# The 32x32 inverses of a delta-rule attention stage on VectorE: one triangular solve of 32 rows, or two of 16 rows and products for the corner

## The chip, the cores and the metric

The kernel runs on one core of a Trainium2 chip. The metric is the time of one execution on the device in microseconds. The core's engines work side by side, each through its own list of instructions in a fixed order: TensorE (matrix products, PE in the profile), VectorE (DVE), ScalarE (ACT), GpSimd (POOL) and SyncE (SP, which here only issues transfers). An instruction that needs another engine's result waits on a semaphore, and everything behind it in its engine's list waits with it.

## What is computed

Three layers in a row, all float32: attention by the delta rule, then two layers of feed-forward networks. Only the first is touched by the change.

```
for t in range(S):                      # S = 768, batch 4, heads 8, head size 48
    y[t]  = q[t] @ state
    v_old = state.T @ k_n[t]            # k_n = k / (|k| + 1e-6)
    state = state + beta[t] * outer(k_n[t], v[t] - v_old)
x = moe(x)                              # 3072 tokens, 8 experts, top 2, 384 -> 1024 -> 384
return (h * clip(h + 3, 0, 6) / 6) @ w_out   # h = x @ w_in, 384 -> 2048 -> 384
```

## The kernel before

The 768 steps of the delta rule are not taken one by one. They are cut into chunks of 64, and a tile `n` holds one chunk of two batches (128 partitions) and all 8 heads; there are 24 tiles. Within a chunk the steps depend on one another through the Gram matrix of the keys, K K^T, below its diagonal. They are resolved at once by the inverse of a unit lower triangular matrix of 64x64 per head. Its two diagonal blocks of 32x32 are inverted on VectorE; the corner is made on TensorE from them (`merge1`, `merge2`).

`gram` multiplies the keys on TensorE into a PSUM tile `gm` (two buffers). ScalarE then reads it: a copy of the corner into `goff`, and a copy, masked to one half, into `gd` (L222, L223). VectorE adds the other half to `gd` (L224; called a Gram sum below) and thereby frees the buffer of `gm` for the Gram after the next. Eight Gram sums (four tiles) fill one `gd`.

`inverse_ops(g)` builds the list of VectorE's work for four tiles, 128 matrices of 32x32: `gd` is transposed into `A` so that each partition holds one whole 32x32 matrix along its free dimension (`A[t, i]`, row t, column i); the norms are made from the diagonal; `A` is scaled (L292); `T` becomes the inverse times the factors in 31 steps. Step jj multiplies column jj of A below the diagonal with row jj of T (L296, `tmp`), and subtracts the product from T below (L304). The subtraction is cut into pieces, so that the next step's row is ready first. Then `T` is transposed into `Xc` and `Yc` (L321, L322). There are six inverses, g = 0 to 5; they are called the first to the sixth below.

For a tile, `merge1` (L347) multiplies `goff` with `Xc`, `merge2` (L368) multiplies with `Yc`, and VectorE assembles the result into `x` (L370, called x below). One PSUM tile `mg` serves both, so the next tile's `merge1` waits for the x before it. `solve` (L399) uses x; `ks` and `update` carry the state from a tile to the tile after next, with ScalarE's copies between them; `output` (L422) makes y. `v_norm` (L377) multiplies v with the norms on GpSimd, two instructions per tile. Tiles two at a time pass through this while the Gram of tiles eight further on is made.

The order is written by hand, apart from VectorE's inverses. These stand in a list with planned costs in us; `run(t)` is called after each piece of TensorE's work with that piece's planned time, times 0.95, and takes from the list what this credit pays for. The tail with the transposes comes when the rest is done. `weave` lays the router's small instructions (`rt_...`) between the inverse's. So a planned cost sets only where in VectorE's list an instruction stands. `late` and `flush` put a Gram sum or an x right behind the piece that made it.

Of the kernel before, what the change touches and what calls it, by code (L numbers as in the profile page):

```python
# [7 lines left out]
F32 = mybir.dt.float32  # L8
# [4 lines left out]
ALU = mybir.AluOpType  # L13
AX = mybir.AxisListType
# [77 lines left out]
def emit_attention(ctx, tc, q, k, v, beta, const, rt, moe):  # L92
    nc = tc.nc
    early = ExitStack()
    pr = early.enter_context(tc.tile_pool(name="at_r", bufs=1, side="right"))
    pk = ctx.enter_context(tc.tile_pool(name="at_k", bufs=1))
    wk = ctx.enter_context(tc.tile_pool(name="at_w", bufs=2))
# [45 lines left out]
    goff, gd, inv, rows, vt, x64, beta_t = {}, {}, {}, {}, {}, {}, {}  # L143
# [59 lines left out]
    def gram(n, hh, what="both"):  # L203
        g, j = divmod(n, 4)
        lo, hi = dict(both=(0, 128), g=(64, 128), m=(0, 64))[what]
        if (j, hh) == (0, 0) and lo < hi and hi == 128:
            gd[g] = pr.tile([128, 32, 32], F32, tag="gd", name="gd", bufs=1)
        if hh == 0 and hi == 128:
            goff[n] = wk.tile([128, NH, 32], F32, tag="goff", name="goff", bufs=11)
        gm = ps2.tile([128, 4, 128], F32, tag="gm", name="gm")  # L210
        for h in range(4):
            for b in range(2):
                m = mq[b][n % NM][st[b], 4 * hh + h]
                nc.tensor.matmul(gm[tok[b], h, lo:hi], lhsT=m[:, 1, :], rhs=m[:, lo // 64:hi // 64, :],  # L214
                                 start=True, stop=True)
        hs = slice(4 * hh, 4 * hh + 4)
        if lo == 0:
            for b in range(2):
                nc.scalar.copy(out=mq[b][n % NM][tok[b], hs, 0, :], in_=gm[tok[b], :, 0:64])
        if hi == 128:  # L220
            d = gd[g][:, 8 * j + 4 * hh:8 * j + 4 * hh + 4, :]
            nc.scalar.mul(out=d, in_=gm[:, :, 64:96], mul=m0)  # L222
            nc.scalar.copy(out=goff[n][:, hs, :], in_=gm[:, :, 64:96])  # L223
            late.append(lambda: nc.vector.scalar_tensor_tensor(  # L224
                out=d, in0=gm[:, :, 96:128], scalar=m1, in1=d, op0=ALU.mult, op1=ALU.add))
        if lo == 0 and hh:
            if n < 6:
                masks.append(n)
            else:
                mask(n)  # L230
# [3 lines left out]
    def mask(n):  # L234
        for b in range(2):
            m = mq[b][n % NM][tok[b], :, 0, :]
            nc.gpsimd.affine_select(out=m, in_=m, pattern=[[0, NH], [1, CH]], compare_op=ALU.is_gt,
                                    fill=0.0, base=0, channel_multiplier=-1)

    def inverse_ops(g):  # L240
        ops = []
        A = pr.tile([128, 32, 32], F32, tag="A", name="A", bufs=1)
        T = pr.tile([128, 32, 32], F32, tag="T", name="T", bufs=1)
        tmp = [pr.tile([128, 256], F32, tag=f"tmp{i}", name="tmp", bufs=1) for i in range(2)]
        sm = wk.tile([128, 8, 32], F32, tag="sm", name="sm", bufs=2)
        rw = wk.tile([128, 32], F32, tag="rows", name="rows", bufs=2)
        rows[g] = rw
        Af, Tf = A.rearrange("p t i -> p (t i)"), T.rearrange("p t i -> p (t i)")
        n2, s, r, nn, gg = [sm[:, i, :] for i in range(5)]

        y, u = sm[:, 5, :], sm[:, 6, :]
        V = nc.vector

        def head():
            nc.gpsimd.memset(T, 0.0)
            V.transpose(out=A, in_=gd[g].rearrange("p j t -> p t j"))
            V.tensor_copy(out=n2, in_=Af[:, 0:1024:33])
            if g == 0:
                nc.scalar.sqrt(s, n2)

        if g == 0:
            norm = [
                lambda: V.tensor_scalar(out=nn, in0=s, scalar1=1e-30, scalar2=None, op0=ALU.add),
                lambda: V.reciprocal(out=r, in_=nn),
                lambda: V.tensor_tensor(out=r, in0=n2, in1=r, op=ALU.mult),
                lambda: V.tensor_tensor(out=s, in0=s, in1=r, op=ALU.add),
                lambda: V.tensor_scalar(out=nn, in0=s, scalar1=0.5, scalar2=1e-6, op0=ALU.mult, op1=ALU.add),
            ]
        else:
            norm = [  # L270
                lambda: V.tensor_scalar(out=u.bitcast(I32), in0=n2.bitcast(I32), scalar1=1, scalar2=None,
                                        op0=ALU.logical_shift_right),
                lambda: V.tensor_scalar(out=y.bitcast(I32), in0=u.bitcast(I32), scalar1=-1.0,
                                        scalar2=float(0x5F3759DF), op0=ALU.mult, op1=ALU.add),
            ] + [
                lambda: V.scalar_tensor_tensor(out=u, in0=y, scalar=-0.5, in1=n2, op0=ALU.mult, op1=ALU.mult),
                lambda: V.tensor_tensor(out=u, in0=u, in1=y, op=ALU.mult),
                lambda: V.scalar_tensor_tensor(out=y, in0=u, scalar=1.5, in1=y, op0=ALU.add, op1=ALU.mult),
            ] * 3 + [
                lambda: V.tensor_tensor(out=s, in0=n2, in1=y, op=ALU.mult),  # L280
                lambda: V.tensor_scalar(out=nn, in0=s, scalar1=1e-6, scalar2=None, op0=ALU.add),
            ]
        norm += [
            lambda: V.tensor_tensor(out=r, in0=nn, in1=nn, op=ALU.mult),
            lambda: V.reciprocal(out=r, in_=r),
            lambda: V.transpose(out=rw, in_=nn),
            lambda: V.tensor_tensor(out=gg, in0=beta_t[g], in1=r, op=ALU.mult),
            lambda: V.tensor_copy(out=Tf[:, 0:1024:33], in_=gg),
        ]

        def scale():
            V.tensor_tensor(out=A, in0=A, in1=gg.unsqueeze(2).to_broadcast([128, 32, 32]), op=ALU.mult)  # L292

        def product(jj):
            m, w = 31 - jj, jj + 1
            nc.vector.tensor_tensor(  # L296
                out=tmp[jj % 2][:, 0:m * w].rearrange("p (t k) -> p t k", k=w),
                in0=A[:, jj + 1:32, jj:jj + 1].to_broadcast([128, m, w]),
                in1=T[:, jj:jj + 1, 0:w].to_broadcast([128, m, w]), op=ALU.mult)

        def subtract(jj, lo, hi):
            if lo < hi:
                w = jj + 1
                nc.vector.tensor_tensor(  # L304
                    out=T[:, lo:hi, 0:w], in0=T[:, lo:hi, 0:w],
                    in1=tmp[jj % 2][:, (lo - w) * w:(hi - w) * w].rearrange("p (t k) -> p t k", k=w), op=ALU.subtract)

        def step(jj):
            product(jj)
            if jj:  # L310
                subtract(jj - 1, (jj + 33) // 2, 32)
            subtract(jj, jj + 1, jj + 2)
            subtract(jj, jj + 2, (jj + 34) // 2)

        def tail():
            if g == NG - 1:
                second()
            X = wk.tile([128, 32, 32], F32, tag="Xc", name="Xc", bufs=1)
            Y = wk.tile([128, 32, 32], F32, tag="Yc", name="Yc", bufs=1)
            inv[g] = (X, Y)  # L320
            nc.vector.transpose(out=X.rearrange("p j t -> p t j"), in_=T)  # L321
            nc.vector.transpose(out=Y.rearrange("p j k -> p k j"), in_=T.rearrange("p t k -> p k t"))  # L322

        ops.append((1.6, head))
        ops.extend((0.23, fn) for fn in norm)
        ops.append((1.1, scale))
        for jj in range(31):
            ops.append((0.25 + 0.0021 * (31 - jj) * (jj + 1), lambda jj=jj: step(jj)))
        ops.append((None, tail))
        return ops  # L330

# [3 lines left out]
    def second():  # L335
        other = ps2.tile([128, NH, 32], F32, tag="gm", name="mg2")
        nc.vector.memset(other, 0.0)
        mgs.update({NT - 3: other, NT - 1: other})
# [187 lines left out]
    for i in range(8):  # L526
        if TA > 1:
            flush()
        if i + TA < 8:
            trans(*divmod(i + TA, 2))  # L530
        flush()
        gram(*divmod(i, 2), "g")
        warm(P1[i])
# [4 lines left out]
    for m in range(4):  # L538
        load_v(m)
        if m < 2:  # L540
            load_k(m)
    pend += inverse_ops(0)
    run(4.0)
    rt.setup(wk, ps2)
    for n in range(4):
        for hh in range(2):
            gram(n, hh, "m")
            warm(P2)
            run(PQ)
    trans(4, 0)  # L550
    for i in range(8, 16):
        n, hh = divmod(i, 2)
# [29 lines left out]
    for n in range(0, NT - 4, 2):  # L582
        a = n + LA
# [84 lines left out]
    n = NT - 4  # L668
# [956 lines left out]
```

## Time and profile before

| | |
|---|---|
| median of 3 runs | 1234.47 us (1234.45 to 1235.84) |
| span of the profiled execution | 1245.6 us |
| TensorE, busy | 1163.7 us (93%) |
| VectorE, busy | 711.4 us (57%) |
| ScalarE, busy | 548.2 us (44%) |
| GpSimd, busy | 311.6 us (25%) |

The profile is of one execution by itself. No other time than its span is recorded for it; the span is 11.1 us longer than the median of the runs. The attention stage takes about the first 345 us; the six inverses begin (transpose of gd into A) at 20.61, 59.15, 108.63, 160.71, 211.95 and 266.61 us, and the last one's transposes end at 313.8 us. A time such as 101.47 is the start of an instruction, in us from the start of the span. The rows below say in brackets how long the engine sat idle before an instruction, and what ended it.

### The profile page before, as it was taken

Reading aid. Unit: us, or ns where it says so; the run is one execution under the profiler, and the core shown is the slowest. Engines: PE = TensorE matmul, PEld = TensorE weight load, DVE = VectorE, ACT = ScalarE, POOL = GpSimd, SP = SyncE. Lnnn points to the kernel's source line nnn. Section 1 sums busy time; section 2 is a strip of 40 time slices with the busy share of each in tenths; the row PEclk is TensorE's granted clock in tenths of the full one; section 3 lists DMA queues with packets and bytes.
Section 4 is the critical chain, followed back from the end, with each engine's and each line's share of the span. In section 5 each row is a group of like instructions: output and inputs, shape, how many; then the busy total and the mean of one; then the engine's idle time right before and its main releaser. Section 6 shows DMA issues by size and latency. Waiting matters only on the chain. (4 is left out here: it accounts for less than half of the span.)

```text
span 1245.6 us, 26717 instructions
## 1 busy us (share of the span) xinstructions
PE 1163.7 (93%) x10743; PEld 1051.9 (84%) x10760; DVE 711.4 (57%) x1923; ACT 548.2 (44%) x1133; POOL 311.6 (25%) x399
## 2 busy tenths in 40 slices
PE   7798888787878999999999999989999999999998
PEld 4476767665757999999999999978989898998988
DVE  7988789879363777675757453436242433425150
ACT  5776777763453433232324233337242433434150
POOL 7242244555244513232231313015000000000000
PEclk9998899988889999999999999999999999999999
DMA  4634334322325545444534321262202010110000
GB/s 85 103 79 92 66 73 92 73 40 42 91 77 190 159 161 173 164 144 155 188 136 160 116 90 56 67 200 78 70 7 64 13 60 17 45 33 2 24 1 26
DMA packets 146530, 109.47 MB, mean 88 GB/s; under 512 B 110104, under 2 KB 131941, under 8 KB 145638
## 3 DMA queue, kind: packets, MB, share of 16 engines
q1 hardware_dynamic: 137446, 86.39, 25.1%
q0 software_dynamic: 8448, 19.70, 4.9%
q8 instruction: 85, 1.39, 0.5%
q10 hardware_dynamic: 512, 1.67, 0.4%
q14 instruction: 39, 0.32, 0.1%
HBM read 82.43 MB, written 26.08 MB: 87 GB/s over the span
## 5 line engine op out<-in xcount | busy, mean ns | idle before, releaser
L1197 PE MATMUL yp<-w2h,ht 128*128 128x384 f32 x832 | 221.2, 340 | 0.0
L1197 PE MATMUL yp<-w2l,ht 128*128 128x384 f32 x448 | 150.2, 335 | 0.0
L1197 PEld LDWEIGHTS yp<-w2h,ht 128*128 128x128 f32 x832 | 148.5, 188 | 0.3
L987 POOL DMA_INDIRECT y<-ys,idp x56 | 65.0, 1161 | 301.8 <-DVE ys L1206 223.5
L1174 PE MATMUL hp<-xth,w1h 128*128 128x416 f32 (+2 forms) x384 | 136.9, 357 | 0.6 <-ACT xth L1115 0.6
L1174 PE MATMUL hp<-xtl,w1h 128*128 128x416 f32 (+2 forms) x384 | 136.2, 355 | 0.0
L1174 PE MATMUL hp<-xth,w1l 128*128 128x416 f32 (+2 forms) x384 | 135.8, 354 | 0.0
L1535 PE MATMUL yp<-woh,gh 128*128 128x384 f32 x384 | 130.4, 340 | 0.0
L1535 PE MATMUL yp<-woh,gl 128*128 128x384 f32 x384 | 129.1, 336 | 0.0
L1535 PE MATMUL yp<-wol,gh 128*128 128x384 f32 x384 | 129.1, 336 | 0.0
L1177 ACT ACTIVATE ht<-hp 128x416 fp32r<-128x416 f32 (+2 forms) x128 | 66.4, 519 | 133.1 <-PE hp L1174 118.4
L1180 DVE SCALAR_TENSOR_TENSOR ht<-hp,ht 128x352 fp32r<-128x352 f32 (+3 forms) x192 | 79.3, 441 | 63.5 <-ACT ht L1177 61.3
L1503 PE MATMUL hp<-xh,wih 128*128 128x512 f32 x288 | 112.8, 392 | 2.7 <-DVE three L1489 2.7
L304 DVE TENSOR_TENSOR T<-T,tmp 128x1 f32<-128x1 f32 (+9 forms) x540 | 113.8, 258 | 0.4
L1503 PE MATMUL hp<-xl,wih 128*128 128x512 f32 x288 | 112.9, 392 | 0.0
L1503 PE MATMUL hp<-xh,wil 128*128 128x512 f32 x288 | 112.7, 391 | 0.0
L1512 DVE TENSOR_TENSOR gl<-r,gh 128x512 fp32r<-128x512 f32 x96 | 66.5, 693 | 78.4 <-ACT gh L1511 78.4
L1506 ACT ACTIVATE r<-hp,three 128x512 f32<-128x512 f32 x96 | 66.2, 690 | 89.0 <-PE hp L1503 89.0
L1508 DVE SCALAR_TENSOR_TENSOR r<-r,hp 128x512 f32<-128x512 f32 x96 | 65.4, 681 | 53.9 <-ACT r L1506 53.9
L1197 PEld LDWEIGHTS yp<-w2l,ht 128*128 128x128 f32 x448 | 84.1, 188 | 0.0
L214 PE MATMUL gm<-mq 64*64 64x128 f32 (+1 forms) x896 | 60.8, 266 | 19.6 <-ACT mq L201 11.0
L1542 ACT ACTIVATE os<-yp 128x384 f32<-128x384 f32 x23 | 11.3, 492 | 153.4 <-PE yp L1535 153.4
(221 smaller groups left out, 2300.5 us busy)
## 6 DMA issues: line engine op xcount, KB each, us to landing
r<-in_moe_w_dram SPq DMA_DIRECT2D x16, 768.0 KB
r<-in_moe_w_dram SPq DMA_DIRECT2D x21, 512.0 KB
yg<-y SPq DMA_DIRECT2D x24, 384.0 KB
wd_r<-in_moe_w_in_dram SPq DMA_DIRECT2D x6, 1024.0 KB
wd_r<-in_moe_w_out_dram SPq DMA_DIRECT2D x8, 768.0 KB
kq<-in_q_dram SPq DMA_DIRECT2D x48, 96.0 KB
kq<-in_k_dram SPq DMA_DIRECT2D x48, 96.0 KB
v<-in_v_dram SPq DMA_DIRECT2D x48, 96.0 KB
```

The lines of the kernel that those rows point to most:

```text
L214: nc.tensor.matmul(gm[tok[b], h, lo:hi], lhsT=m[:, 1, :], rhs=m[:, lo // 64:hi // 64, :], start=True, stop=True)
L304: nc.vector.tensor_tensor(out=T[:, lo:hi, 0:w], in0=T[:, lo:hi, 0:w], in1=tmp[jj % 2][:, (lo - w) * w:(hi - w) * w].rearrange("p (t k) -> ...
L987: return nc.gpsimd.indirect_dma_start(out=y, out_offset=bass.IndirectOffsetOnAxis(ap=idx, axis=0), in_=src, in_offset=None, bounds_check=y ...
L1174: nc.tensor.matmul(p[:, 0:w], lhsT=a[:, k, fs], rhs=b[:, k, c], start=(i == 0), stop=(i == 3 * KD - 1))
L1177: nc.scalar.activation(out=h[:, c], in_=p[:, 0:w], func=ACTF.Relu)
L1180: nc.vector.scalar_tensor_tensor(out=h[:, rest(lo, hi)], in0=p[:, lo - c.start:hi - c.start], scalar=0.0, in1=h[:, lo:hi].bitcast(F32), op ...
L1197: nc.tensor.matmul(p[0:2 * m if pair else m, 0:DM], lhsT=a, rhs=b[:, f, :], start=f == i == 0, stop=f == FT - 1 and i == len(terms) - 1)
L1503: nc.tensor.matmul(p, lhsT=a[:, k, fs], rhs=b[:, k, :], start=(i == 0), stop=(i == 3 * KD - 1))
L1506: nc.scalar.activation(out=r, in_=p, func=ACTF.Relu, bias=three)
L1508: nc.vector.scalar_tensor_tensor(out=r, in0=r, scalar=6.0, in1=p, op0=ALU.min, op1=ALU.mult)
L1512: nc.vector.tensor_tensor(out=gl[:, f, :], in0=r, in1=gh[:, f, :].bitcast(F32), op=ALU.subtract)
L1535: nc.tensor.matmul(p[:, 0:DM], lhsT=a[:, f, c], rhs=b[:, f, :], start=(i == 0), stop=(i == 3 * FT2 - 1))
```

## The change

The inverse of a 32x32 triangular matrix is made from its 16x16 blocks. The two diagonal blocks are inverted side by side, by the same steps as before, but 15 of them, and each instruction holds both blocks (the pattern `blocks` picks them from A and T by one stride of 528 elements). The lower left block is then minus the inverse of the lower block, times A's lower left block, times the inverse of the upper. `left(q)` makes the second of these products for four columns: one instruction writes all single products, read by broadcasting, into scratch space (`big`, or a part of `A` no longer needed), a second one (TENSOR_REDUCE) sums them over the last axis into `GT`. `right(q)` does the same for four rows with the inverse of the lower block. The two tiles `tmp` become one that also holds `GT`. New planned costs go with it. In `gram` the copy into goff stands before the masked copy into gd.

```
-        A = pr.tile([128, 32, 32], F32, tag="A", name="A", bufs=1)
-        T = pr.tile([128, 32, 32], F32, tag="T", name="T", bufs=1)
-        tmp = [pr.tile([128, 256], F32, tag=f"tmp{i}", name="tmp", bufs=1) for i in range(2)]
+        Af = pr.tile([128, 1056], F32, tag="A", name="A", bufs=1)
+        Tf = pr.tile([128, 1056], F32, tag="T", name="T", bufs=1)
+        A, T = [t[:, 0:1024].rearrange("p (t i) -> p t i", i=32) for t in (Af, Tf)]
+        Ab, Tb = blocks(Af), blocks(Tf)
+        scratch = pr.tile([128, 256], F32, tag="tmp", name="tmp", bufs=1)
...
         def product(jj):
-            m, w = 31 - jj, jj + 1
+            m, w = 15 - jj, jj + 1
+            V.tensor_tensor(
+                out=part(jj, w, 16), in0=Ab[:, :, w:16, jj:w].to_broadcast([128, 2, m, w]),
+                in1=Tb[:, :, jj:w, 0:w].to_broadcast([128, 2, m, w]), op=ALU.mult)
...
+        def left(q):
+            w = 16 - 4 * q
+            t = (big[:, 0:1024], big[:, 0:768], Af[:, 0:512], big[:, 768:1024])[q].rearrange(
+                "p (t j k) -> p t j k", t=16, j=4)
+            mult = lambda: V.tensor_tensor(
+                out=t, in0=A[:, 16:32, 4 * q:16].unsqueeze(2).to_broadcast([128, 16, 4, w]),
+                in1=T[:, 4 * q:16, 4 * q:4 * q + 4].rearrange("p k j -> p j k").unsqueeze(1).to_broadcast(
+                    [128, 16, 4, w]), op=ALU.mult)
+            add = lambda: V.tensor_reduce(out=GT[:, 4 * q:4 * q + 4, :].rearrange("p j t -> p t j"), in_=t, axis=AX.X,
+                                          op=ALU.add)
+            return 0.1 + 0.046 * w, mult, add
+
+        def right(q):
+            w = 4 * q + 4
+            t = (big if q % 2 else Af)[:, 0:64 * w].rearrange("p (t j k) -> p t j k", t=4, j=16)
+            rows4 = slice(16 + 4 * q, 20 + 4 * q)
+            mult = lambda: V.tensor_tensor(
+                out=t, in0=T[:, rows4, 16:16 + w].unsqueeze(2).to_broadcast([128, 4, 16, w]),
+                in1=GT[:, :, 0:w].unsqueeze(1).to_broadcast([128, 4, 16, w]), op=ALU.mult)
+            add = lambda: V.tensor_reduce(out=T[:, rows4, 0:16], in_=t, axis=AX.X, op=ALU.add, negate=True)
+            return 0.1 + 0.046 * w, mult, add
...
-        ops.append((1.1, scale))
-        for jj in range(31):
-            ops.append((0.25 + 0.0021 * (31 - jj) * (jj + 1), lambda jj=jj: step(jj)))
+        ops.append((0.7, scale))
+        ops.extend((0.42, lambda jj=jj: step(jj)) for jj in range(15))
+        for side in left, right:
+            parts = [side(q) for q in range(4)]
+            a, b, c, d = (0, 2, 1, 3) if side == left else (3, 2, 1, 0)
+            order = [(a, 1), (b, 1), (a, 2), (c, 1), (b, 2), (d, 1), (c, 2), (d, 2)]
+            ops.extend((parts[q][0], parts[q][i]) for q, i in order)
...
+            nc.scalar.copy(out=goff[n][:, hs, :], in_=gm[:, :, 64:96])
             nc.scalar.mul(out=d, in_=gm[:, :, 64:96], mul=m0)
-            nc.scalar.copy(out=goff[n][:, hs, :], in_=gm[:, :, 64:96])
```

Where instructions stand on an engine. In these pieces L296, L304 are the steps of before and L309, L316 those of the changed kernel; L329 and L333 are products and sums of the left side, L341 and L344 those of the right. L370 is the x of before, L406 that of the changed kernel; `rt_` are the router's.

VectorE in the fourth inverse, around the first x; before:

```order
L875 MAX rt_mx<-rt_t 128x8
L296 TENSOR_TENSOR tmp<-A,T 128x252
L304 TENSOR_TENSOR T<-T,tmp 128x7x17
L304 TENSOR_TENSOR T<-T,tmp 128x18
L304 TENSOR_TENSOR T<-T,tmp 128x6x18
L875 MAX rt_mx<-rt_t 128x8
L224 SCALAR_TENSOR_TENSOR gd<-gm,half,gd 128x128
L370 SCALAR_TENSOR_TENSOR x_3350<-Xc,half,mg 128x8x32
L296 TENSOR_TENSOR tmp<-A,T 128x247
```

The same place after:

```order
L329 TENSOR_TENSOR big<-A,T 128x256
L911 MAX rt_mx<-rt_t 128x8
L333 TENSOR_REDUCE tmp<-big 128x16x4
L912 MAX_INDEX rt_mi<-rt_mx,rt_t 128x8
L333 TENSOR_REDUCE tmp<-big 128x16x4
L912 MAX_INDEX rt_mi<-rt_mx,rt_t 128x8
L341 TENSOR_TENSOR big<-T,tmp 128x1024
L912 MAX_INDEX rt_mi<-rt_mx,rt_t 128x8
L224 SCALAR_TENSOR_TENSOR gd<-gm,half,gd 128x128
L406 SCALAR_TENSOR_TENSOR x_3209<-Xc,half,mg 128x8x32
L341 TENSOR_TENSOR A<-T,tmp 128x768
```

Before, 18 of the 31 steps stand ahead of this x; after, all 15 steps, the left side and one product of the right side.

VectorE at the end of the second inverse, up to the transpose that begins the third; before:

```order
L304 TENSOR_TENSOR T<-T,tmp 128x30
L296 TENSOR_TENSOR tmp<-A,T 128x31
L304 TENSOR_TENSOR T<-T,tmp 128x30
L304 TENSOR_TENSOR T<-T,tmp 128x31
L224 SCALAR_TENSOR_TENSOR gd<-gm,half,gd 128x128 x2
L321 STREAM_TRANSPOSE Xc<-T 128x32x32
L322 STREAM_TRANSPOSE Yc<-T 128x32x32
L256 STREAM_TRANSPOSE A<-gd 128x1024
```

The same place after:

```order
L341 TENSOR_TENSOR A<-T,tmp 128x256
L224 SCALAR_TENSOR_TENSOR gd<-gm,half,gd 128x128
L344 TENSOR_REDUCE T<-big 128x4x16
L344 TENSOR_REDUCE T<-A 128x4x16
L353 STREAM_TRANSPOSE Xc<-T 128x32x32
L354 STREAM_TRANSPOSE Yc<-T 128x32x32
L224 SCALAR_TENSOR_TENSOR gd<-gm,half,gd 128x128 x3
L263 STREAM_TRANSPOSE A<-gd 128x1024
```

The two transposes of the result stand ahead of the last three Gram sums, where they stood behind all of them.

ScalarE behind a Gram; before:

```order
L219 COPY mq_137<-gm 64x4x64
L219 COPY mq_147<-gm 64x4x64
L222 ACTIVATE gd<-gm,half 128x128
L223 COPY goff<-gm 128x128
L201 COPY mq_138<-tp 64x512
```

After:

```order
L219 COPY mq_137<-gm 64x4x64
L219 COPY mq_147<-gm 64x4x64
L222 COPY goff<-gm 128x128
L223 ACTIVATE gd<-gm,half 128x128
L201 COPY mq_138<-tp 64x512
```

The two copies have changed places; nothing else moves on ScalarE.

## Rows read from the trace of the kernel before

**Rows 1.** Busy time by stretch: length; PE, PEld, DVE, ACT, POOL; granted clock; DMA share, GB/s.
```profile
160.70:211.90 51.20, 43.33 (x1023) 35.72 (x1025) 44.63 (x187) 39.86 (x98) 25.43 (x39) 0.97 0.44 80
430.00:1245.00 815.00, 805.98 (x4338) 764.01 (x4336) 388.54 (x670) 288.42 (x523) 123.53 (x107) 1.00 0.27 88
```

**Rows 2.** TensorE's waits up to 345 us: us in total, times, longest.
```profile
PE mg L347 <- DVE x L370: 7.3, 6, 3.5
PE gm L214 <- DVE gd L224: 6.8, 5, 3.0
...
PE mg L347 <- DVE Xc L321: 2.6, 1, 2.6
...
PE tpx L821 <- DVE gap L805: 2.2, 1, 2.2
```

**Rows 3.** TensorE in order of time: start, us, instruction, [idle before <-releaser].
```profile
101.47 1.97 PE L214 MATMUL gm<-mq 64*64 64x128 f32 x16 [3.02 <-DVE gd L224]
192.02 0.69 PE L347 MATMUL mg<-Xc,goff 32*32 32x32 f32 x32 [0.89 <-DVE x L370]
242.92 0.69 PE L347 MATMUL mg<-Xc,goff 32*32 32x32 f32 x32 [1.42 <-DVE x L370]
244.13 1.09 PE L214 MATMUL gm<-mq 64*64 64x128 f32 x16
297.26 0.90 PE L821 MATMUL tpx<-ident,x 128*128 128x128 f32 x3 [2.21 <-DVE gap L805]
301.62 1.06 PE L347 MATMUL mg<-Xc,goff 32*32 32x32 f32 x32 [3.46 <-DVE x L370]
```

**Rows 4.** VectorE in order of time, in four inverses; columns as in rows 3.
```profile
26.12 1.22 DVE L292 TENSOR_TENSOR A<-A,sm 128x1024 f32<-128x1024 f32 x1
27.37 0.21 DVE L296 TENSOR_TENSOR tmp<-A,T 128x31 f32<-128x31 f32 x1
...
75.01 0.22 DVE L296 TENSOR_TENSOR tmp<-A,T 128x60 f32<-128x60 f32 x1
75.15 0.79 DVE L304 TENSOR_TENSOR T<-T,tmp 128x15 f32<-128x15 f32 x3
...
103.36 0.19 DVE L296 TENSOR_TENSOR tmp<-A,T 128x31 f32<-128x31 f32 x1
...
188.59 0.42 DVE L296 TENSOR_TENSOR tmp<-A,T 128x256 f32<-128x256 f32 x1
188.93 0.55 DVE L304 TENSOR_TENSOR T<-T,tmp 128x120 f32<-128x120 f32 x3
...
211.62 0.22 DVE L911 TENSOR_REDUCE rt_sf<-rt_oh 128x8 f32<-128x64 f32 x1
```

**Rows 5.** A stretched product, and lines L377, L321: ns min/median/max, first and last start.
```profile
37.31 1.05 DVE L296 TENSOR_TENSOR tmp<-A,T 128x256 f32<-128x256 f32 x1
...
L377 POOL TENSOR_TENSOR us<-v,rows x48: 820/837/1436, 37.1 to 317.3; 64x384 f32<-64x384 f32 x48
...
L321 DVE STREAM_TRANSPOSE Xc<-T x6: 1897/1928/1967, 55.6 to 310.1; 128x1024 f32<-128x1024 f32 x6
```

**Rows 6.** VectorE in the second and third inverse, in order of time.
```profile
88.86 0.35 DVE L224 SCALAR_TENSOR_TENSOR gd<-gm,half,gd 128x128 f32<-128x128 f32 x1 [0.72 <-ACT goff L223]
...
139.31 0.48 DVE L370 SCALAR_TENSOR_TENSOR x<-Xc,half,mg 128x256 f32<-128x256 f32 x1 [1.36 <-ACT rz L155]
...
145.51 0.35 DVE L224 SCALAR_TENSOR_TENSOR gd<-gm,half,gd 128x128 f32<-128x128 f32 x1 [2.08 <-ACT goff L223]
```

**Rows 7.** ScalarE's pair behind one Gram, and the sum on VectorE that waits for it.
```profile
124.78 0.37 ACT L222 ACTIVATE gd<-gm,half 128x128 f32<-128x128 f32 x1
125.05 0.26 ACT L223 COPY goff<-gm 128x128 f32<-128x128 f32 x1
...
125.34 0.35 DVE L224 SCALAR_TENSOR_TENSOR gd<-gm,half,gd 128x128 f32<-128x128 f32 x1 [1.82 <-ACT goff L223]
```

**Rows 8.** A stretch after the wait at 101.47; columns as in rows 1.
```profile
99.30:109.50 10.20, 7.09 (x83) 5.76 (x85) 9.45 (x28) 3.80 (x11) 3.55 (x5) 0.50 0.11 32
```

More of the change, by code (lines that the diff above doesn't have):

```diff
@@ L238, in mask, with blocks @@
                                     fill=0.0, base=0, channel_multiplier=-1)
+    big = pr.tile([128, 1024], F32, name="big")
+    def blocks(t):
+        return t.rearrange("p (s r) -> p s r", s=2)[:, :, 0:512].rearrange("p s (t k) -> p s t k", k=32)[:, :, :, 0:16]
     def inverse_ops(g):
         ops = []
-        A = pr.tile([128, 32, 32], F32, tag="A", name="A", bufs=1)
-        T = pr.tile([128, 32, 32], F32, tag="T", name="T", bufs=1)
-        tmp = [pr.tile([128, 256], F32, tag=f"tmp{i}", name="tmp", bufs=1) for i in range(2)]
-        sm = wk.tile([128, 8, 32], F32, tag="sm", name="sm", bufs=2)
+        Af = pr.tile([128, 1056], F32, tag="A", name="A", bufs=1)
[3 more added lines that the diff above has]
+        scratch = pr.tile([128, 256], F32, tag="tmp", name="tmp", bufs=1)
+        tmp = [scratch[:, 128 * i:128 * i + 128] for i in range(2)]
+        GT = scratch.rearrange("p (j t) -> p j t", j=16)
+        sm = wk.tile([128, 5, 32], F32, tag="sm", name="sm", bufs=2)
         rw = wk.tile([128, 32], F32, tag="rows", name="rows", bufs=2)
         rows[g] = rw
-        Af, Tf = A.rearrange("p t i -> p (t i)"), T.rearrange("p t i -> p (t i)")
         n2, s, r, nn, gg = [sm[:, i, :] for i in range(5)]
-        y, u = sm[:, 5, :], sm[:, 6, :]
+        y, u = gg, r
         V = nc.vector
         def head():
-            nc.gpsimd.memset(T, 0.0)
+            nc.gpsimd.memset(Tf[:, 0:1024], 0.0)
             V.transpose(out=A, in_=gd[g].rearrange("p j t -> p t j"))
@@ L291, in scale, with part @@
         def scale():
-            V.tensor_tensor(out=A, in0=A, in1=gg.unsqueeze(2).to_broadcast([128, 32, 32]), op=ALU.mult)
-        def product(jj):
-            m, w = 31 - jj, jj + 1
[L296 to L299, printed above, removed]
+            V.tensor_tensor(out=Ab, in0=Ab, op=ALU.mult,
+                            in1=gg.rearrange("p (s t) -> p s t", s=2).unsqueeze(3).to_broadcast([128, 2, 16, 16]))
+        def part(jj, lo, hi):
+            w = jj + 1
+            t = tmp[jj % 2][:, 0:2 * (16 - w) * w].rearrange("p (s t k) -> p s t k", s=2, k=w)
+            return t[:, :, lo - w:hi - w]
+        def product(jj):
+            m, w = 15 - jj, jj + 1
+            V.tensor_tensor(
+                out=part(jj, w, 16), in0=Ab[:, :, w:16, jj:w].to_broadcast([128, 2, m, w]),
+                in1=Tb[:, :, jj:w, 0:w].to_broadcast([128, 2, m, w]), op=ALU.mult)
         def subtract(jj, lo, hi):
             if lo < hi:
[L303 to L306, printed above, removed]
+                t = Tb[:, :, lo:hi, 0:jj + 1]
+                V.tensor_tensor(out=t, in0=t, in1=part(jj, lo, hi), op=ALU.subtract)
         def step(jj):
@@ L310, in step @@
             if jj:
[L311 removed]
+                subtract(jj - 1, (jj + 17) // 2, 16)
             subtract(jj, jj + 1, jj + 2)
[L313 removed]
+            subtract(jj, jj + 2, (jj + 18) // 2)
+        def left(q):
[18 more added lines that the diff above has]
+            return 0.1 + 0.046 * w, mult, add
         def tail():
```

## The prediction

> **What bounds the kernel now.** I read the stretches first. From 430 us to the end TensorE is busy 805.98 of 815.00 us and VectorE 388.54 [rows 1]: nothing of the change runs there, and it only starts earlier or later. In the attention stage, here the stretch of the fourth inverse (160.7 to 211.9 us), TensorE is busy 43.33 of 51.20 us and VectorE 44.63: neither is full, and each waits for the other. So the question is where TensorE waits for VectorE. The waits of TensorE up to 345 us give it: 7.3 us for the merged block x (six times), 6.8 us for the Gram sum gd (five times), 2.6 us for the first transposed inverse Xc, 2.2 us for the router's gap, 18.9 us together [rows 2]. TensorE's order in time shows the largest of them [rows 3]: 3.02 us before the Gram at 101.47, 0.89 before the merge at 192.02, 1.42 at 242.92, 2.21 and 3.46 at 297.26 and 301.62. In all of these VectorE had inverse steps queued ahead of the small instruction that TensorE needed. What counts is therefore less what an inverse costs than how much of it stands ahead of each gd and x.
>
> **What an inverse costs.** A product of 60 elements starts its successor 0.14 us later (75.01 to 75.15), one of 256 elements 0.34 us later (188.59 to 188.93) [rows 4]: about 0.08 us for an instruction and 1.04 ns for an element. Before, an inverse has 121 of them with 2 x 5456 elements: 121 x 0.08 + 10912 x 0.00104 = 9.7 + 11.3 = 21.0 us. After, the two 16x16 blocks take 56 instructions with 2 x 1360 elements: 4.5 + 2.8 = 7.3 us. The left side adds four products of 1024, 768, 512 and 256 elements (0.3 + 2.7 = 3.0 us) and four sums over as many, the right side the same. The only sum over an axis in the trace, 64 elements, took 0.22 us [rows 4], where the law of the products gives 0.08 to the next start and the instruction lasts about 0.08 longer: the same rate, so 3.0 us for each four sums. Bounds of a large sum: not under the 1.04 ns of the products; at most the 1.93 us of a transpose of 1024 elements [rows 5], which would add 0.84 ns x 5120 = 4.3 us per inverse.
>
> The left products read T down its columns, 128 bytes from one element to the next. The first step of before reads a column of 31 elements once and takes 0.21 us, the last step a row of 31 and takes 0.19 [rows 4]: some 0.5 ns more an element, so 2560 x 0.5 = 1.3 us (bounds 0, and 2.7 if each element costs twice). The Trainium skill (SBUF — State Buffer, the note on cachelines in "Door 1: The DMA port swizzle") says that elements in different 16-byte lines each pay a penalty; it gives no price. The rows agree in sign.
>
> Scaling falls from 1024 to 512 elements; the row of before has 1.22 us [rows 4], so 0.6 less. Sum: 7.3 + 3.0 + 1.3 + 3.0 + 6.0 - 0.6 = 20.0 against 21.0. VectorE's own work falls by 1.0 us per inverse (bounds: 2.3 less without the column price, 4.7 more with slow sums and double columns). This alone decides little, since VectorE is not full.
>
> **What stands ahead of gd and x.** Fourth inverse, first x: before, 18 of 31 steps stand ahead (70 instructions, about 6600 elements): 5.6 + 6.9 = 12.5 us. After, all steps, the left side and the first right product: 7.3 + 4.3 + 3.0 + 1.1 = 15.7, less 0.6 for scaling: 2.6 us more. Second x: before 86 instructions and 8490 elements, 15.7 us; after 19.6 - 0.6: 3.3 us more. At the end of the second inverse the last three Gram sums also get the two transposes of the result ahead of them, which were behind. The plan counts a left or right instruction of 1024 elements as 0.84 us where the law gives 1.14, so more work is issued early than VectorE has done by then. Behind each such gd or x on VectorE stand the router's small instructions and the rest of the inverse; on TensorE the merge, the solve and the update, thus the whole chain.
>
> In us that TensorE gets later, inverse by inverse:
> First: the four Gram sums come 3 to 4 later, but the wait of 2.6 for Xc goes, since the transposes are issued before the last three sums; +0.5.
> Second: 3.1 later at the sum of 88.86, less 0.7 that VectorE idles there [rows 6] and 1.0 of earlier start; the later sum at 100.98 gains nothing more, as the transposes that now stand ahead take the place of instructions that GpSimd held; +1.5.
> Third: 2.6 later at x, but VectorE idles 1.36 us there and 2.08 at the next sum [rows 6]; +1.0.
> Fourth: no idle there; TensorE already waits 0.89 at 192.02; +2.5.
> Fifth: the same place with 1.42 of wait, less about 0.6 for one GpSimd instruction that meets a sum instead of a product; +2.0.
> Sixth: the gap 2.8 later and x 3.6, where TensorE waits 2.21 and 3.46 already [rows 3], less 1.2 for GpSimd; +2.5.
> Sum +10.0 us. I take it whole, because each wait stands in a chain that the next tile needs; the GpSimd relief is in the terms already.
>
> The exchange of goff and gd on ScalarE I cost at nothing. The sum at 125.34 starts when the second of the pair (125.05, 0.26 us) has ended, not the first (124.78, 0.37) [rows 7]; the pair ends at the same time in either order. If not, it is 0.26 us either way at a sum that TensorE waits for; five did [rows 2], 1.3 us. The counts of TensorE, ScalarE, GpSimd and SyncE don't change; only in the fourth and fifth inverse the router's two rank products go ahead of the last Gram of the group. Their input, the router's count, stands ahead of the second x on VectorE, done by then, so this is for nothing; if not, it is one more wait of under 1 us in each.
>
> **The time.** The profiled execution has a span of 1245.6 us, 11.1 above the median of the three runs, 1234.47. On the profile's scale I expect 1255.6, on the runs' scale 1244.5. The likeliest case's own range is 1238.5 to 1249.5: half the terms absorbed, or half again as much.
>
> **Rivals.**
> 1. Absorbed, no change. VectorE waits often for ScalarE before a sum, and the 2.08 us of [rows 6] show that later work can fall into such gaps. For it: the third inverse. Against it: in the second, fourth, fifth and sixth there is no idle where TensorE waits. If all terms fall away, and 1.0 us per inverse hardly shows: 1234.5.
> 2. Faster, through GpSimd. GpSimd's product of v took 0.84 us 48 times, and a VectorE product that meets it lasts 1.05 us in place of 0.42 [rows 4, 5]. At 0.63 each this is 30 us of VectorE's time. Transposes stayed between 1.90 and 1.97 us [rows 5]: an instruction with one input is not held. The sums have one input and are 6 of the 20 us; if GpSimd's products mostly meet sums or wait behind a long product, 12 to 15 us go, over 2 us per inverse, which with the 1.0 saved cancels the lateness at x and takes a third of the 18.9 us of waits: 1228.5. It decides from 2.6 us of relief before x; but in the fourth inverse the largest product ahead of x ran its plain 0.42 us at 188.59 [rows 4], so there is little to win just there. The Trainium skill (SBUF — State Buffer, "Who interferes with whom") says that tensor_reduce never contends and that a product with two SBUF inputs contends with GpSimd's reads; the rows agree for the products, and no row here shows a reduce beside GpSimd.
> 3. Slower still. After TensorE's 3.02 us of waiting the granted clock was 0.50, the 1.2 GHz level, from 99.3 to 109.5 [rows 8], and a Gram took 1.97 us (101.47) in place of 1.09 (244.13) [rows 3]. If each of four lengthened waits brings 3.4 us at that level, about 1.5 us each, and the columns cost double (1.4 us more at five places), it is 10 + 6 + 7, part of it hidden, say 18: 1252.5. It decides once the waits at 192 and 243 pass some 2 us.
>
> **Chances.** Forecast 0.53, absorbed 0.13, faster 0.17, slower still 0.17. A difference under 0.2% (2.5 us) can't be told from none. Slower: 0.53 + 0.17 and a little of the absorbed case, 0.71. Same: 0.09. Faster: 0.17 and a little of the absorbed case, 0.20. The range 1230 to 1254 holds the forecast, the absorbed case, half of the slower one and the upper edge of the faster one. The large-sum bound of 4.3 us per inverse would reach past it and is given little.
>
> **What would show it.** Right: sums of 1024 elements at 1.1 to 1.2 us, left products near 1.7, right ones near 1.2; an undisturbed inverse near 20 us; TensorE's waits for x and gd well above 14 us, with 3 us or more at the fourth inverse's merge; the wait for Xc gone. Wrong: sums or products much under 1 ns an element, v products of GpSimd no longer stretching VectorE, or TensorE's waits for VectorE at or under 18.9 us while the stage from 20 to 345 us is not longer. Sums waiting other than before for ScalarE would undo the zero of the exchange.

## The result, and the profile after

The changed kernel takes 1249.1 us (five runs, 1248.0 to 1251.3) where the kernel before takes 1233.6 in the same set: a ratio of 1.0125, interval 1.0103 to 1.0147. An earlier set gave 1249.1 against 1234.6, 1.0117 (1.0083 to 1.0150); a fourth run of that set, of 2808 us, was in a slow state and is left out. So the change costs about 15 us; 10 were forecast. The times of before differ between the sets of experiments (1233.6 in the first, 1244.1 and 1244.8 in the other two), so kernels of different sets are compared by their ratio to before.

The kernel before was profiled again beside the kernel after, with spans of 1231.2 and 1249.5 us: these two traces differ by 18.3 us, near what the runs differ by. The first trace of the kernel after spans 1243.6 us and that of before 1245.6, so a single execution of each need not show the loss. The stretches, as in [rows 1]; first two of before, then three of after (the fourth inverse, 164.3 to 218.6, answers to 160.7 to 211.9 of [rows 1]):

```profile
20.00:345.00 325.00, 269.81 (x5843) 215.06 (x5858) 270.98 (x1111) 221.00 (x533) 137.12 (x205) 0.91 0.40 83
430.00:1245.00 815.00, 792.67 (x4267) 750.96 (x4265) 375.19 (x652) 281.06 (x511) 118.27 (x103) 1.00 0.25 85
```
```profile
20.00:345.00 325.00, 259.59 (x5646) 209.25 (x5657) 250.27 (x776) 211.73 (x514) 142.34 (x199) 0.90 0.39 74
164.30:218.60 54.30, 41.87 (x996) 35.03 (x997) 42.73 (x140) 39.75 (x97) 27.33 (x39) 0.94 0.46 76
430.00:1245.00 815.00, 810.54 (x4363) 768.41 (x4361) 391.22 (x674) 289.10 (x526) 124.73 (x109) 1.00 0.27 89
```

From 20 to 345 us VectorE is busy 250.3 us in place of 271.0, and TensorE got through less: 259.6 us of work in place of 269.8. Both engines wait more. The late part (430 on) only starts later; the 815 us there hold more of it because the trace is longer. The fourth inverse's stretch is 54.3 us, where the second trace of before has 52.0 for it (157.7 to 209.7). TensorE's waits up to 345 us, before and after (us in total, times, longest):

```profile
PE gm L214 <- DVE gd L224: 6.6, 5, 3.0
PE mg L347 <- DVE x L370: 6.5, 6, 3.5
PE mg L347 <- DVE Xc L321: 2.6, 1, 2.6
PE tpx L821 <- DVE gap L805: 2.2, 1, 2.2
```
```profile
PE mg L383 <- DVE x L406: 20.2, 7, 5.5
PE gm L214 <- DVE gd L224: 7.8, 5, 3.1
PE tpx L857 <- DVE rt_pos L943: 5.6, 1, 5.6
```

The wait for x has tripled, the one for Xc has gone, gd is little changed. A wait of 5.6 us for the router's positions (rt_pos, the slot of every token; 0.6 us before) has come in place of the gap. TensorE in order of time, after, against [rows 3]:

```profile
142.96 1.07 PE L383 MATMUL mg<-Xc,goff 32*32 32x32 f32 x32 [3.57 <-DVE x L406]
145.00 1.97 PE L214 MATMUL gm<-mq 64*64 64x128 f32 x16
199.34 1.06 PE L383 MATMUL mg<-Xc,goff 32*32 32x32 f32 x32 [5.45 <-DVE x L406]
253.57 0.69 PE L383 MATMUL mg<-Xc,goff 32*32 32x32 f32 x32 [3.98 <-DVE x L406]
300.44 0.90 PE L857 MATMUL tpx<-ident,x 128*128 128x128 f32 x3 [5.59 <-DVE rt_pos L943]
312.76 1.06 PE L383 MATMUL mg<-Xc,goff 32*32 32x32 f32 x32 [4.16 <-DVE x L406]
```

Third, fourth, fifth and sixth inverse, each with 3.6 to 5.6 us at its x or positions. What VectorE did before the one at 199.34 (the fourth inverse; start, us, instruction):

```profile
187.23 2.22 DVE L329 TENSOR_TENSOR big<-A,T 128x1024 f32<-128x1024 f32 x1
189.35 0.85 DVE L909 TENSOR_TENSOR rt_t<-rt_t,nz 128x32 f32<-128x32 f32 x1
190.12 1.08 DVE L329 TENSOR_TENSOR A<-A,T 128x512 f32<-128x512 f32 x1
191.88 1.21 DVE L333 TENSOR_REDUCE tmp<-big 128x64 f32<-128x1024 f32 x1
193.12 1.48 DVE L329 TENSOR_TENSOR big<-A,T 128x768 f32<-128x768 f32 x1
...
197.30 1.20 DVE L341 TENSOR_TENSOR big<-T,tmp 128x1024 f32<-128x1024 f32 x1
...
198.82 0.47 DVE L406 SCALAR_TENSOR_TENSOR x<-Xc,half,mg 128x256 f32<-128x256 f32 x1
```

The whole left side and the first right product run before x, without a gap, as the order said.

### The profile page after: what moved, and what is told of

Read it like the earlier page. It is cut to its first block, busy times and chain, and to the rows that moved or that the text cites. A ratio compares the mean times of both kernels' runs of the same rounds, so it can differ in the third digit from the quotient of the medians.

```text
span 1243.6 us, 26427 instructions
## 1 busy us (share of the span) xinstructions
PE 1157.8 (93%) x10744; PEld 1051.0 (85%) x10760; DVE 699.9 (56%) x1635; ACT 549.0 (44%) x1133; POOL 324.6 (26%) x399
## 5 line engine op out<-in xcount | busy, mean ns | idle before, releaser
L214 PEld LDWEIGHTS gm<-mq 64*64 64x64 f32 x896 | 48.3, 143 | 34.6 <-ACT mq L201 13.6
```

## The experiments

Theory A is the prediction's: what the plan puts ahead of each x and gd on VectorE decides, more than the inverse's length. Its rivals are named in the expectations.

**1. The kernel before once more.**

> The kernel before, unchanged, profiled once more, to have its trace beside that of the kernel after on one chip. Theory A (what stands ahead of gd and x decides): about 1234.5 us, TensorE's waits for x and gd near 14 us together as in the first trace, which was 11 us longer than its timed runs for a reason outside the change (more half-clock stretches). Rival B (the time hangs on the clock's stretches alone): a profile near 1234 us has the same waits for x and gd as the kernel after, and only fewer half-clock stretches.

Measured: 1234.5 us, span 1231.2; the waits for x and gd are 13.1 us, as in [rows 2]. B falls: a shorter trace has the same waits as the longer one, not those of the kernel after. The 14 us by which the first trace of before is longer than this one lie elsewhere, partly in the clock. The stretch from 130 to 140 us, first trace and second:

```profile
130.00:140.00 10.00, 9.18 (x172) 7.86 (x170) 8.64 (x39) 5.11 (x13) 1.87 (x3) 0.50 0.13 44
```
```profile
130.00:140.00 10.00, 8.44 (x249) 7.21 (x247) 10.00 (x47) 7.37 (x19) 2.04 (x3) 1.00 0.13 44
```

The granted clock is 0.50 (1.2 GHz) in the one and 1.00 (2.4 GHz) in the other.

**2. The kernel after once more.**

> The kernel after, unchanged. 1246 to 1251 us; ratio to before 1.010 to 1.013. A: TensorE waits 21 to 25 us for x and gd up to 350 us, 8 to 10 more than before; the largest at the first x of the fourth, fifth and sixth inverse. B: waits within 3 us of before's, half-clock stretches 20 us longer in sum.

Measured: 1249.1 us, 1.0125 (1.0103 to 1.0147). Waits for x and gd 28.0 us, 14.9 more than before; more than A expected, and at the places that it named, plus the third inverse. In the first trace of the kernel after they are 23.0 us (14.8 and 8.2), within what A expected. B's other sign is missing too: from 20 to 345 us TensorE ran at half clock for 65 us in this trace and 51 in the first, against 58 and 61 in the two of before.

**3. The exchange on ScalarE undone.**

```
-            nc.scalar.copy(out=goff[n][:, hs, :], in_=gm[:, :, 64:96])
             nc.scalar.mul(out=d, in_=gm[:, :, 64:96], mul=m0)
+            nc.scalar.copy(out=goff[n][:, hs, :], in_=gm[:, :, 64:96])
```

> The kernel after with ScalarE's pair behind each Gram in the old order (gd scaled first, then goff copied). Theory A with the exchange at nothing: within 1.5 us of the kernel after. Rival C (the exchange makes the Gram sum wait one copy longer, 0.26 us at some 21 waits of VectorE, a part of them on TensorE's path): 2 to 5 us faster than the kernel after, and VectorE's wait for ScalarE before the sum falls from some 33 to some 21 us.

Measured: 1251.6 us, 1.0141 (1.0117 to 1.0166), 2.5 us over the kernel after, a little more than the 1.5 expected; the intervals overlap, so no difference can be told. VectorE's longest wait in total, up to 345 us, with the exchange undone and as changed:

```profile
DVE gd L224 <- ACT goff L223: 40.5, 26, 4.0
```
```profile
DVE gd L224 <- ACT gd L223: 41.7, 25, 4.0
```

The sum waits for the second of ScalarE's pair in either order. The growth from 20.8 us (18 times) before is not the exchange's; C falls.

**4. The plan's costs as measured.**

```
-            return 0.1 + 0.046 * w, mult, add                            (in left and in right)
+            return (0.15 + 0.113 * w, 0.12 + 0.067 * w), mult, add       (left: product, sum)
+            return (0.12 + 0.067 * w, 0.12 + 0.067 * w), mult, add       (right)
-        ops.extend((0.42, lambda jj=jj: step(jj)) for jj in range(15))
+        ops.extend((0.49, lambda jj=jj: step(jj)) for jj in range(15))
-            ops.extend((parts[q][0], parts[q][i]) for q, i in order)
+            ops.extend((parts[q][0][i - 1], parts[q][i]) for q, i in order)
```

Of the inverse's 96 instructions on VectorE, 87 stand ahead of the first x in the fourth inverse of the kernel after, 81 here; ahead of the second 92 and 85. That is six fewer at the first x, where four were expected.

> The kernel after with the plan's costs set to durations of its trace: a step 0.49 instead of 0.42, a left product of width w 0.15 + 0.113 w, every other left or right instruction 0.12 + 0.067 w, instead of 0.1 + 0.046 w for all. The work is the same; at the fourth inverse three left instructions and one right product (2.9 us) come behind the first x instead of ahead of it. A (what stands ahead decides): 5 to 10 us faster than the kernel after, 1240 to 1245 us, TensorE's waits for x down by 5 us or more. Rival D (VectorE's work as such, or its collisions with GpSimd, decides): within 2 us of the kernel after, the lateness returning at the next Gram sums and at the next inverse.

Measured: 1236.5 us, 1.0025 (1.0006 to 1.0045) on the chip of experiments 1 to 3. That is 12.5 of the 15 us back, more than expected, with the same instructions. TensorE's waits up to 345 us:

```profile
PE mg L383 <- DVE x L406: 11.4, 7, 2.8
PE mg L383 <- DVE Xc L353: 5.8, 4, 4.2
PE rk L940 <- POOL rt_acc L933: 5.5, 1, 5.5
PE tpx L857 <- DVE rt_pos L943: 3.6, 1, 3.6
...
PE gm L214 <- DVE gd L224: 0.9, 2, 0.7
```

x is down by 8.8 us and the longest wait from 5.5 to 2.8, and gd from 7.8 to 0.9. In exchange 5.8 us of wait for Xc come, since the end of the inverse, with its transposes, is issued later, and 5.5 for the router. All of TensorE's waits for VectorE and GpSimd together fall by only some 3 us, so the time follows those for x and gd and not their sum. D falls.

**5. The same error in the kernel before.**

```
-            ops.append((0.25 + 0.0021 * (31 - jj) * (jj + 1), lambda jj=jj: step(jj)))
+            ops.append((0.8 * (0.25 + 0.0021 * (31 - jj) * (jj + 1)), lambda jj=jj: step(jj)))
```

> The kernel before with the planned costs of its inverse steps times 0.8; work, code and instructions unchanged. In the fourth inverse 21 of 31 steps stand ahead of the first x in place of 18 and 28 in place of 22 ahead of the second (by the durations about 2.5 and 4 us), and the transposes of the result go ahead of the last Gram sums: about the share by which the kernel after counts its instructions too cheap against the kernel before. A (what stands ahead decides, whatever the inverse is made of): 6 to 15 us slower than before (ratio 1.005 to 1.012), waits for x and gd up by 6 us or more. Rival F (the new instructions themselves, long products against GpSimd, cost the time): within 2 us of the kernel before.

Measured: 1258.8 us where before takes 1244.8, 1.0121 (1.0103 to 1.0138): the loss of the change itself, without one of its instructions. F falls. TensorE's waits up to 345 us, and the longest:

```profile
PE mg L347 <- DVE x L370: 14.4, 4, 5.5
PE gm L214 <- DVE gd L224: 4.8, 2, 4.3
```
```profile
252.87 1.06 PE L347 MATMUL mg<-Xc,goff 32*32 32x32 f32 x32 [5.53 <-DVE x L370]
```

Experiments 4 and 5 together show the cause from both sides: costs put right in the new kernel take most of the loss away, costs put wrong in the old one bring it. The waits for x and gd together rose by 6.1 us, the lower end of what was expected, since gd fell. The mean granted clock from 20 to 345 us fell with it, to 0.87 from 0.91, with 85 us of the stretch at half clock in place of 58:

```profile
20.00:345.00 325.00, 269.31 (x5553) 211.85 (x5548) 257.18 (x1060) 208.97 (x510) 131.34 (x198) 0.87 0.38 74
```

How the loss of this run divides between waits and clock is not shown.

**6. TensorE kept busy in the waits.**

```
+            warm(14 if n % 4 == 2 and n > 2 else 0)
             live(merge1, n + 1)
```

> The kernel after with 14 more of the kernel's warming products on TensorE (about 0.21 us each, 3 us) ahead of the merge that waits for x in the third to sixth inverse. Nothing else changes; the waits for x become shorter by as much as the products fill, x itself does not come earlier. If the half-clock stretches behind these four waits carry part of the loss: 3 to 8 us faster than the kernel after, granted clock 1.00 behind the waits. If they carry nothing, or only move: within 2 us of the kernel after or slower.

Measured: ratio 1.0100 (1.0067 to 1.0133), against 1.0125 (1.0103 to 1.0147) in another set: inconclusive. The wait for x fell as meant, but the stage's mean clock did not rise (0.90 from 20 to 345 us in both kernels):

```profile
20.00:345.00 325.00, 274.37 (x5505) 211.95 (x5505) 245.54 (x768) 208.38 (x508) 140.55 (x195) 0.90 0.38 71
```
```profile
PE mg L383 <- DVE x L406: 4.8, 3, 2.3
```

The 14 products fill the wait and do not end it: 15.4 us less of it in the table of waits, and hardly any in the time. What the half-clock stretches carry of the 15 us stays open.

**7 and 8. The left products along rows.** In 7 they are written with strides:

```
-                out=t, in0=A[:, 16:32, 4 * q:16].unsqueeze(2).to_broadcast([128, 16, 4, w]),
-                in1=T[:, 4 * q:16, 4 * q:4 * q + 4].rearrange("p k j -> p j k").unsqueeze(1)...
+                out=t.rearrange("p t j k -> p t k j"),
+                in0=A[:, 16:32, 4 * q:16].unsqueeze(3).to_broadcast([128, 16, w, 4]),
+                in1=T[:, 4 * q:16, 4 * q:4 * q + 4].unsqueeze(1).to_broadcast([128, 16, w, 4])
```

> The kernel after with its left products read along T's rows (inner loop over j, A broadcast) and written into the same scratch layout with strides, sums unchanged. Same work, order and planned costs. If the column read is what makes the left product of 1024 elements 1.96 us and not 1.2: products of 1.2 to 1.3 us, 2.0 us less VectorE ahead of x in every inverse, and by theory A 3 to 8 us faster than the kernel after (1241 to 1246). Rival E (a strided write costs as much as the column read did): 1.9 us again, and within 2 us of the kernel after.

In 8 the products are written in that order, [t, k, j], and the sums read them with strides (`in_=t.rearrange("p t k j -> p t j k")`).

> As before it, but the left products are written in order and the four sums read them with strides of 16 bytes. Tells where a stride costs: product 1.2 us, and the sum of 1024 elements 1.2 us if reading with a stride of 16 bytes is free, up to 2.0 us if it costs what the column did.

Measured: 1.0120 (1.0088 to 1.0152), no gain; E holds. Experiment 8, run once and not compared, took 1267.6 us. By shape (mean ns of one behind the comma): the kernel after with its contiguous right product and sum below, then 7, then 8:

```profile
L329 DVE TENSOR_TENSOR big<-A,T 128x1024 f32<-128x1024 f32 x6 | 12.4, 2075 | 0.1
L341 DVE TENSOR_TENSOR big<-T,tmp 128x1024 f32<-128x1024 f32 x6 | 7.5, 1255 | 0.0
L333 DVE TENSOR_REDUCE tmp<-big 128x64 f32<-128x1024 f32 x6 | 7.3, 1212 | 0.0
```
```profile
L329 DVE TENSOR_TENSOR big<-A,T 128x1024 f32<-128x1024 f32 x6 | 11.5, 1908 | 0.1
```
```profile
L333 DVE TENSOR_REDUCE tmp<-big 128x64 f32<-128x1024 f32 x6 | 12.0, 2007 | 0.0
L329 DVE TENSOR_TENSOR big<-A,T 128x1024 f32<-128x1024 f32 x6 | 7.4, 1226 | 0.1
```

The stride costs some 0.65 to 0.8 ns an element in each of the three places: read by the product at 128 bytes (2075 - 1255 over 1024), written at 64 (1908 - 1255), read by the sum at 16 (2007 - 1212). The means of products hold some stretching by GpSimd; by the shortest of the six (1916 and 1192 ns) the first is 0.71.

**9. Without the lower left corner.**

```
-        for side in left, right:
+        for side in ():
```

> The kernel after without the left and right instructions (the lower left 16x16 block of each inverse stays zero): some 15 us less VectorE work per inverse, all else in place. Bounds what the inverse's length can cost at all. A: TensorE's waits for x, gd and the router's positions (33 us in the kernel after) go nearly all, and the stretches at half clock behind them: 20 to 35 us faster than the kernel after, 1215 to 1230. Rival B (clock and other engines set the attention stage): not faster than the kernel before, 1233 or more.

This kernel leaves the corner out and so computes something else; it is run for its time alone. Measured: 0.9894 (0.9860 to 0.9927): 2.3% under the kernel after, some 28 us. A holds, and the run gives a price: 15 us per inverse, 90 in all, taken off VectorE are worth 28, some 0.3 us for each, even with everything ahead of x shortened. TensorE no longer waits for x or gd; its largest wait is one for ScalarE, and the clock stays at 0.96:

```profile
20.00:345.00 325.00, 274.94 (x5920) 216.50 (x5914) 181.70 (x748) 227.19 (x547) 137.71 (x216) 0.96 0.41 82
```
```profile
PE gm L214 <- ACT mq L201: 11.8, 25, 1.7
```

**10 to 12. Versions meant to beat both.** Measured costs with the rows of 7, left products planned as 0.12 + 0.067 w:

> Measured costs and rows together (left products planned at 0.12 + 0.067 w). A: the two gains overlap, because the costs alone brought the time to 1236.5; 1 to 4 us faster than with measured costs alone, 1232 to 1236, about the kernel before or a little under it. E: 1236 to 1240, no gain, since a left product planned at 1.2 us would last 1.9.

Measured: 0.9986 (0.9965 to 1.0007), the same as before. The left product of 1024 elements took 1.92 us, as E had it, and the time came out at the better end of A's. So planning it at 1.19 us did no harm here: a single cost that is too low need not lose time, and the waits for x and gd were 10.1 us in all.

Measured costs, and halving adds in place of the left sums (products as in 8; here `m` is half of the `h` partial sums left):

```
+                    V.tensor_tensor(out=o, in0=t[:, :, 0:m, :], in1=t[:, :, h - m:h, :], op=ALU.add)
```

> Measured costs, and a left side without strides: products written in order (k outside, j inside) and each sum as halving adds of contiguous runs, 13 adds of 2304 elements in place of 4 sums of 2560. By the law 13 x 0.08 + 2304 x 0.00104 = 3.4 us for 3.0, and products 3.0 for 5.0: 1.5 us less VectorE per inverse than with measured costs alone. A: 2 to 6 us faster than measured costs, 1231 to 1235 on a chip where before takes 1233.6, ratio 0.996 to 1.000. Rival F (two-input instructions meet GpSimd): no gain, ratio 1.002 to 1.005.

> As tree_costs with the planned costs from the scaling on times 1.12, so that about 1 us more of the inverse comes behind each x and gd. A says less waiting for x and gd, but the result's transposes come later, so that the wait for Xc grows: within 3 us of tree_costs, on either side.

Measured: 1.0009 (0.9991 to 1.0028), between what A and F expected, and, planned 12% dearer, 1.0030 (1.0009 to 1.0052), within 3 us of it as expected. No version is faster than before. The halving adds cost more than the law gave. The left product of 1024 elements, and VectorE's adds behind it:

```profile
L329 DVE TENSOR_TENSOR big<-A,T 128x1024 f32<-128x1024 f32 x6 | 8.0, 1331 | 0.1
```
```profile
133.79 1.46 DVE L339 TENSOR_TENSOR big<-big 128x512 f32<-128x512 f32 x3
135.28 0.27 DVE L339 TENSOR_TENSOR tmp<-big 128x64 f32<-128x64 f32 x1
```

The product is down to 1.33 us, but its four adds take 1.76 us, where the law of the prediction gives 4 x 0.08 + 960 x 0.00104 = 1.32 and the one strided sum of 8 took 2.01 and the contiguous sum of the kernel after 1.21. Rival F, stretching by GpSimd, has a part in it: of the six such chains two took 1.46 us for the first three adds, the other four 1.81 to 2.54. It is not the whole, since the two unstretched ones are over the law as well, by some 0.1 us for each add, which needs the one before it; why was not tried.

## Why the prediction was right, and where its steps failed

**The direction and the mechanism.** Less VectorE work, and later x: both as said, and experiments 4 and 5 show that the order makes the loss. The size was forecast too small: the 15 us lie between the forecast's 10 and the 18 of rival 3, at the upper edge of the likeliest case's own range (1249.5). "The plan counts a left or right instruction of 1024 elements as 0.84 us" was the sentence that mattered, though it stood as a remark beside the sum: the whole of steps, left and right stands in the plan at 15 x 0.42 + 4 x (0.4 + 0.046 x 40) = 15.3 us; by the durations it is 7.3 (steps, by the law) + 5.4 (left products) + 3.4 (right) + 6.4 (sums) = 22.5. Before, the plan had 31 x 0.25 + 0.0021 x 5456 = 19.2 us for 21.0. So the new work is counted about a quarter too cheap beside the old; with GpSimd's stretching, from each start to the next in the traces, it is 23.2 us after and 24.9 before, and some 15% too cheap.

**Waits and time.** The waits of TensorE's merge for x and of its Gram for gd, up to 345 us, in one trace of each kernel, beside the ratio of its runs to before:

| kernel | x and gd, us | ratio |
|---|---|---|
| without the corner (9) | 1.0 | 0.9894 |
| measured costs, rows (10) | 10.1 | 0.9986 |
| halving adds (11) | 12.3 | 1.0009 |
| measured costs (4) | 12.3 | 1.0025 |
| before (1) | 13.1 | 1.0005 |
| halving adds, dearer (12) | 15.2 | 1.0030 |
| before, costs too low (5) | 19.2 | 1.0121 |
| rows (7) | 26.0 | 1.0120 |
| exchange undone (3) | 26.7 | 1.0141 |
| after (2) | 28.0 | 1.0125 |

A microsecond of these waits goes with about one of time (28.0 - 1.0 us with 2.3%, 28 us). Experiment 5 lies above that, with its lower clock, and experiment 6 (12.7 us, 1.0100) is left out because TensorE's waits are filled there.

**The terms, inverse by inverse.** Lateness added in each, from the start of one inverse's transpose of A to the next (the first from the start of the span, the sixth to the first activation of the feed-forward), against the second trace of before: two executions of the kernel after, and in the last column the first trace of before itself:

| inverse | forecast | after, first | after, second | before, first |
|---|---|---|---|---|
| first | +0.5 | +0.5 | +0.5 | +0.2 |
| second | +1.5 | -1.8 | -0.8 | -0.2 |
| third | +1.0 | +3.2 | +6.9 | +3.0 |
| fourth | +2.5 | +1.0 | +2.3 | -0.8 |
| fifth | +2.0 | +1.3 | +0.8 | +0.7 |
| sixth | +2.5 | +5.9 | +8.2 | +9.2 |
| sum | +10.0 | +10.1 | +17.9 | +12.1 |

The third and the sixth came out larger than forecast, the second smaller. That the first execution's sum meets the forecast is luck, since its terms do not. And the last column shows that one kernel differs from itself by 3.0 us in the third inverse and 9.2 in the sixth, so these traces do not size the two terms; what they show is the waits there.

Third: the step "VectorE idles 1.36 us there and 2.08 at the next sum" failed. That idle time was read in the trace whose clock is 0.50 from 130 to 140 us (experiment 1); that TensorE was late for this reason, and VectorE waited, fits but is not shown apart. In the second trace of before, where the clock is 1.00, VectorE comes to the same x and the same next sum without such a cushion, with no idle time and 0.38 us in place of 1.36 and 2.08:

```profile
138.04 0.47 DVE L370 SCALAR_TENSOR_TENSOR x<-Xc,half,mg 128x256 f32<-128x256 f32 x1
...
142.51 0.35 DVE L224 SCALAR_TENSOR_TENSOR gd<-gm,half,gd 128x128 f32<-128x128 f32 x1 [0.38 <-ACT goff L223]
```

With 11 us of left side and router between the Gram sum at 130.79 and the one at 142.19, TensorE waited 3.57 us at 142.96, and half clock came with it, with a Gram of 1.97 us at 145.00. The clock behind that wait, and over the same stage of before:

```profile
140.00:150.00 10.00, 7.04 (x113) 5.79 (x114) 8.30 (x25) 3.48 (x10) 2.33 (x4) 0.58 0.54 102
```
```profile
136.00:146.00 10.00, 9.91 (x262) 8.43 (x262) 9.62 (x50) 8.02 (x20) 3.50 (x5) 1.00 0.30 57
```

Sixth: the sum had the gap and x, not the router's positions. In the order on VectorE 68 of 144 instructions of the inverse stood ahead of them; now it is 79 of 96, all the steps and the first left product:

```profile
298.37 1.92 DVE L329 TENSOR_TENSOR big<-A,T 128x1024 f32<-128x1024 f32 x1
300.20 0.19 DVE L943 TENSOR_TENSOR rt_pos<-rk,ebase 128x32 f32<-128x32 f32 x1
```

TensorE stood 5.59 us for it, in the first trace of the kernel after 5.6 as well; x then cost 4.16, near the 3.46 of before [rows 3]. The term for the gap (2.2 us before) had to be one for the positions.

**The durations.** Sums of 1024 elements 1.21 us and right products 1.25: as worked out. Left products 2.08 on the average and 1.92 at the least, where about 1.7 was worked out: the column price was taken at 0.5 ns an element, and is 0.7 to 0.8, inside the bounds; 0.5 to 0.8 us more per inverse. Experiments 7 and 8 correct the reason as well: it is no matter of columns, each stride that was tried (16, 64 and 128 bytes) cost it. The Trainium skill (SBUF — State Buffer, the note on cachelines in "Door 1: The DMA port swizzle") speaks of 16-byte lines, and the sum's 2007 ns at just 16 bytes agree with it.

**The exchange at nothing:** held (experiment 3).

**Rival 1, absorbed:** only in the second inverse.

**Rival 2, GpSimd's relief:** its mechanism came, and not its sign. The time by which steps, scaling, products and sums exceed 1.05 times the lower quartile of their shape comes to 24.5 us in the second trace of before and 11.1 after: some 13 us of relief, where the rival said 12 to 15. But GpSimd's own instructions got longer. Its v products, before and after:

```profile
L377 POOL TENSOR_TENSOR us<-v,rows 64x384 f32<-64x384 f32 x48 | 41.9, 873 | 23.7 <-DVE T L304 11.5 <-DMA ids<-pair,slots 4.1 <-DMA kbd<-in_k_dram 3.8
```
```profile
L413 POOL TENSOR_TENSOR us<-v,rows 64x384 f32<-64x384 f32 x48 | 51.8, 1078 | 28.5 <-DMA v<-in_v_dram 11.5 <-DMA ids<-pair,slots 7.4 <-DMA kbd<-in_k_dram 3.9
```

And VectorE's time was not what decided: by the price of experiment 9 such 13 us are worth some 4, an estimate. Of the twelve sums of 1024 elements in the second trace of the kernel after, three ran beside v products for nearly their whole length, and all twelve took 1.19 to 1.23 us. The Trainium skill (SBUF — State Buffer, "Who interferes with whom") says that tensor_reduce never contends on trn2; the trace agrees.

**Rival 3, half clock behind the waits:** the waits at 199.34 and 253.57 passed its 2 us (a figure that no run tried), and half clock came with each of the five waits shown above: the mean clock over the 10 us from 142, 199, 252, 300 and 312 is 0.51, 0.80, 0.83, 0.73 and 0.66. The stage of before has nearly as much of it at other places (experiment 2), so that the mean over the whole stage hardly changed (0.91 and 0.90). Experiment 6 could not part the clock from the wait, so how much of the 5 us over the forecast is this rival's stays open.

## What to carry to other kernels

Where a plan of costs spreads one engine's long work between another engine's small, urgent instructions, new instructions need costs as true as the old ones had: some 15 to 25% too cheap lost 1.2% here, in either kernel. Read idle time that is to absorb something from a stretch at full clock, or from two executions. Look for every instruction that the other engine waits for behind the moved work, the router's positions as well as the merge.

## What the runs showed of the hardware

- A stride in one operand of a 1024-element VectorE instruction cost 0.65 to 0.8 us: a product's input read at 128 bytes, its output written at 64, a sum's input read at 16 (experiments 7 and 8).
- Long two-input products on VectorE hold GpSimd's: two v products, 0.84 us each at the median, took 4.19 us together beside the left products at 187.23 and 190.12. The router's 32-element instruction between these two on VectorE (189.35, above) took 0.85 us, where its like at 186.87 took 0.18:

```profile
187.71 4.19 POOL L413 TENSOR_TENSOR us<-v,rows 64x384 f32<-64x384 f32 x2
```
